# Seven quarter products for the last four MLP blocks of an attention and MLP kernel

## The chip, the cores and the metric

The kernel runs on one core of one Trainium2 chip. The metric is the time of the program on the device in microseconds (us), median over runs; lower is better. Before: 1475.31 us, median of three runs (1474.25 to 1478.08).

In the profiles PE is the matrix engine and PEld its loading of weights, DVE is the vector engine, ACT the scalar engine and POOL a fourth one; PSUM is the memory that matmuls add into, in banks. A record is one instruction of the trace; each matmul of the MLP shows as two records (2304 of hT in the page of before, for 18 blocks of 64 matmuls). Tile names: sc is the scores, xT the attention weights times V (a "weighing"), hT a piece of h, g its Gelu, o_ps the second MLP product, and bank a PSUM tile of the changed kernel.

## The reference, cut to what matters

Attention with a threshold (batch 8, 8 heads, 576 tokens, head size 64), then a two-layer MLP with exact Gelu over the 4608 tokens. All data is 32-bit floating point in the kernel; the MLP weights come in as 64-bit and are converted there.

```python
scores = scale * np.matmul(q, k.transpose(0, 1, 3, 2))
thresh = np.max(scores, axis=-1, keepdims=True) - tau
scores = np.where(scores >= thresh, scores, -1000000000.0)
attn = softmax(scores)                            # cut
x = (attn @ v).transpose(0, 2, 1, 3).reshape(4608, 512)
h = x @ w_in                                      # 512 x 2048
g = 0.5 * h * (1.0 + erf(h * inv_sqrt2))
return g @ w_out                                  # 2048 x 512
```

## The kernel before

Attention goes in 160 slots: a pair of heads, 128 rows at a time. In each slot the MLP fills the rest of PE's time: `fill` emits MLP matmuls until a "goal", a number of MLP blocks that should be done by then, is met. A block is 256 tokens; there are 18.

```python
def block_steps(n):
    g = {}
    for j in range(N_DF):                          # 16 chunks of d_ff
        if j % 2 == 0:
            hT = None
        for c in range(N_DM):                      # 4 pieces of d_model
            yield NS_IN, (j * P // PIECE + 1) * N_DM
            if hT is None:
                hT = ps.tile([P, 2, TOK], FP32, tag="mm", name="hT")
            nc.tensor.matmul(hT[:, j % 2, :], lhsT=w_in_sb[c][:, j * P:(j + 1) * P], rhs=x_blk[n][:, c, :],
                             start=(c == 0), stop=(c == N_DM - 1))
        if j % 2:
            late.append((g, j, hT))
            gelus(lag[0])                          # up to 2 Gelus stay unissued until the next slot
    for m in range(TOK // P):
        for j in range(N_DF):
            ...                                    # cut
            nc.tensor.matmul(o[:, 0:d_model], lhsT=g[j][:, m * P:(m + 1) * P], rhs=w_out_sb[j],
                             start=(j == 0), stop=(j == N_DF - 1))
        ...                                        # copy to o_sb, write out

GOAL += [(BATCH * (m + 2) + WEIGH, x) for m, x in enumerate([1.96, 3.96, 5.96, 8.06, 10.16, 12.26, 14.36])]
...
for n in range(len(slots) + WEIGH + 1):
    if p < NP:
        scores(p, i)
        softmax_head(p, i)
    gelus(0)                                       # the Gelus left over from the slot before
    table()
    if p > EARLY and i == WEIGH:                   # attention weights times V for the pair before:
        for h in range(2):                         # each half takes one of the four "mm" buffers of PSUM
            weigh_v(p - 1, h * HALF, (h + 1) * HALF)
    ...                                            # softmax_tail, transposes
    fill(owed, tokens)
fill(1e12, B * S)                                  # what is left of the MLP: the tail
```

## Time and profile before

| | before |
|---|---|
| timed runs | 1475.31 us (1474.25 to 1478.08) |
| span of the profile | 1472.4 us |
| PE, DVE, ACT busy | 97%, 63%, 44% |
| last attention matmul ends | 1264.8 us |
| plain MLP after it | 203.8 us |

The prediction below shows the busy shares, the slices and the chain. Two lines of the groups and one of the groups by form complete them. The columns are line, engine, operation, output and inputs, shapes and count, then busy us and the mean ns of one, then the idle time before them.

```profile
L468 PE MATMUL hT<-x,w_in 128*128 128x256 f32 x2304 | 518.7, 382 | 0.0
L480 PE MATMUL o_ps<-w_out,g 128*128 128x512 f32 x1152 | 517.8, 600 | 0.0
...
L428 ACT COPY x<-xT 128x256 f32<-128x256 f32 x20 | 7.4, 371 | 0.8 <-PE xT L419 0.8
```

Both MLP products have no idle time before them, and they overlap: the 382 and 600 ns of one are longer than the distances at which they start (215.9 and 429.2 ns, from the chain). A matmul's price is therefore read from the chain or from a long window, not from the mean of one.

### The profile page before, as it was taken

Reading aid. Unit: us, or ns where it says so; the run is one execution under the profiler, and the core shown is the slowest. Engines: PE = TensorE matmul, PEld = TensorE weight load, DVE = VectorE, ACT = ScalarE, POOL = GpSimd, SP = SyncE. Lnnn points to the kernel's source line nnn. Section 1 sums busy time; section 2 is a strip of 40 time slices with the busy share of each in tenths; the row PEclk is TensorE's granted clock in tenths of the full one; section 3 lists DMA queues with packets and bytes.
Section 4 is the critical chain, followed back from the end, with each engine's and each line's share of the span. In section 5 each row is a group of like instructions: output and inputs, shape, how many; then the busy total and the mean of one; then the engine's idle time right before and its main releaser. Section 6 shows DMA issues by size and latency. Waiting matters only on the chain.

```text
span 1472.4 us, 18592 instructions
## 1 busy us (share of the span) xinstructions
PE 1429.3 (97%) x6288; PEld 904.8 (61%) x6288; DVE 931.8 (63%) x2098; ACT 642.6 (44%) x1014; POOL 294.3 (20%) x502
## 2 busy tenths in 40 slices
PE   6899899999999999999999999999999999999998
PEld 5576447465665657474747575656656665675774
DVE  5988889987777777766676767776766765000000
ACT  5768536546263626352434444354535263210110
POOL 3221324322222222112222222212122000000000
PEclk9999999999999999999999999999999999999999
DMA  9876468886565556556666655545566444000000
GB/s 286 258 262 170 122 118 134 140 143 103 102 107 98 100 100 104 101 89 110 112 112 113 112 103 82 106 86 105 86 112 105 95 81 86 10 15 15 0 15 14
DMA packets 421292, 155.11 MB, mean 105 GB/s; under 512 B 399952, under 2 KB 404624, under 8 KB 421200
## 3 DMA queue, kind: packets, MB, share of 16 engines
q1 hardware_dynamic: 394992, 96.77, 38.8%
q0 software_dynamic: 23808, 56.57, 14.8%
q8 instruction: 51, 0.84, 0.2%
q10 hardware_dynamic: 2400, 0.59, 0.2%
q14 instruction: 41, 0.34, 0.1%
HBM read 61.85 MB, written 9.44 MB: 48 GB/s over the span
## 4 chain that ended last, share of the span: by engine, by line
PE 85%; DVE 7%; ACT 4%; DMA 2%; SPq 2%; issue 1%; DVEq 0%; ACTq 0%
PE o_ps L480 33%; PE hT L468 31%; PE sc L340 11%; PE xT L419 9%; DVE nmx L351 2%; DVE p L365 1%; DMA q<-in_q_dram 1%; ACT p L352 1%; ACT L448 1%; SPq L228 1%; DVE power L176 1%; PE tr L286 1%; DVE pd L393 1%; ACT L455 1%; DMA pT<-pd 0%
## 5 line engine op out<-in xcount | busy, mean ns | idle before, releaser
L468 PE MATMUL hT<-x,w_in 128*128 128x256 f32 x2304 | 518.7, 382 | 0.0
L480 PE MATMUL o_ps<-w_out,g 128*128 128x512 f32 x1152 | 517.8, 600 | 0.0
L468 PEld LDWEIGHTS hT<-x,w_in 128*128 128x128 f32 x2304 | 432.9, 190 | 88.4 <-issue 31.0
L352 ACT ACTIVATE p<-sc,nmx 128x576 f32<-128x576 f32 x288 | 203.2, 741 | 515.9 <-DVE nmx L351 515.8
L480 PEld LDWEIGHTS o_ps<-w_out,g 128*128 128x128 f32 x1152 | 215.2, 191 | 260.9 <-issue 257.7
L351 DVE TENSOR_REDUCE nmx<-sc 128x1 f32<-128x576 f32 x288 | 205.7, 751 | 234.3 <-PE sc L340 234.1
L365 DVE SCALAR_TENSOR_TENSOR p<-sc,thr,p 128x576 f32<-128x576 f32 x288 | 225.4, 816 | 33.1 <-ACT p L352 19.9
L210 POOL DMA_DIRECT2D q<-in_q_dram x104 | 70.0, 679 | 647.5 <-DVE q_tail L328 401.9
L340 PE MATMUL sc<-kT,qT 64*128 64x288 f32 x960 | 158.0, 435 | 14.6 <-DVE p L365 14.3
L419 PE MATMUL xT<-pT,v 128*64 128x288 f32 (+2 forms) x1280 | 165.2, 411 | 4.8 <-ACT g L448 4.8
L393 DVE STREAM_TRANSPOSE pd<-p 128x576 f32<-128x576 f32 x224 | 160.4, 754 | 1.7 <-ACT p L379 1.3
L340 PEld LDWEIGHTS sc<-kT,qT 64*128 64x128 f32 x960 | 87.7, 188 | 91.5 <-issue 76.1
L419 PEld LDWEIGHTS xT<-pT,v 128*64 128x64 f32 x1280 | 90.7, 137 | 75.4 <-issue 14.7
L381 DVE TENSOR_SCALAR p<-p,rden 128x576 f32<-128x576 f32 x240 | 120.2, 536 | 4.9
L218 POOL DMA_DIRECT2D v<-in_v_dram x208 | 111.1, 536 | 60.4 <-DMA k<-in_k_dram 35.4
L448 ACT ACTIVATE g<-hT 128x512 f32<-128x512 f32 x144 | 82.2, 596 | 80.9 <-PE hT L468 79.9
L448 ACT ACT_TABLE_LOAD x81 | 103.9, 1283 | 1.4
L455 ACT ACT_TABLE_LOAD x80 | 102.6, 1283 | 1.4
L483 ACT COPY o_sb<-o_ps 128x512 f32<-128x512 f32 x36 | 20.9, 582 | 138.1 <-PE o_ps L480 134.1
L210 POOL DMA_DIRECT2D k<-in_k_dram x104 | 72.7, 705 | 0.0
L286 PE MATMUL tr<-diag,p 128*128 128x128 f32 (+1 forms) x360 | 47.9, 296 | 8.5 <-ACT g L448 4.6
L286 PEld LDWEIGHTS tr<-diag,p 128*128 128x128 f32 (+1 forms) x360 | 40.7, 190 | 17.7 <-ACT g L448 6.0
(74 smaller groups left out, 551.8 us busy)
## 6 DMA issues: line engine op xcount, KB each, us to landing
pT<-pd SPq DMA_DIRECT2D x448, 160.0 KB, 4.8
out_dram<-o_sb SPq DMA_DIRECT2D x36, 256.0 KB, 2.5
pT<-pd_tail SPq DMA_DIRECT2D x112, 80.0 KB, 2.9
q<-in_q_dram POOLq DMA_DIRECT2D x104, 72.0 KB, 4.6
k<-in_k_dram POOLq DMA_DIRECT2D x104, 72.0 KB, 6.2
v<-in_v_dram POOLq DMA_DIRECT2D x156, 40.0 KB, 5.0
raw<-in_moe_w_out_dram POOLq DMA_DIRECT2D x10, 512.0 KB, 5.5
shifted<-in_moe_w_out_dram POOLq DMA_DIRECT2D x10, 511.5 KB, 5.5
```

The costliest lines, as they stand in the source:

```text
L210: eng.dma_start(t[e * D + f:e * D + f + Q], rows[:, :, f:f + Q])
L340: nc.tensor.matmul(sc[e][:, h, 0:HALF], lhsT=lhsT, rhs=s["kT"][rows, at:at + HALF], start=True, stop=True)
L351: nc.vector.tensor_reduce(nmx[:, e:e + 1], sc, axis=AXIS.XY, op=ALU.max, negate=True)
L352: nc.scalar.activation(w[:, e * S:(e + 1) * S].rearrange("p (h s) -> p h s", h=2), sc, AF.Exp, bias=nmx[:, e:e + 1], scale=1.0)
L365: nc.vector.scalar_tensor_tensor(row, sc[e][:, :, 0:HALF], thr[:, e:e + 1], row, op0=ALU.is_ge, op1=ALU.mult, accum_out=den[:, e:e + 1])
L381: nc.vector.tensor_scalar(row, row, rden[:, e:e + 1], None, op0=ALU.mult)
L393: nc.vector.transpose(to[:, 0:NB, :], w[:, e * S:(e + 1) * S].rearrange("p (b i) -> p b i", i=Q))
L419: nc.tensor.matmul(xT[f, 0:hi - lo], lhsT=s["v"][:, e, c, :], rhs=pT[:, c, lo:hi], start=(c == 0), stop=(c == KR - 1))
L448: nc.scalar.activation(t, hT, AF.Gelu)
L455: nc.scalar.activation(warm[:, 1:2], warm[:, 0:1], AF.Exp)
L468: nc.tensor.matmul(hT[:, j % 2, :], lhsT=w_in_sb[c][:, j * P:(j + 1) * P], rhs=x_blk[n][:, c, :], start=(c == 0), stop=(c == N_DM - 1))
L480: nc.tensor.matmul(o[:, 0:d_model], lhsT=g[j][:, m * P:(m + 1) * P], rhs=w_out_sb[j], start=(j == 0), stop=(j == N_DF - 1))
```

## The change

The last four blocks go two at a time (512 tokens) through Strassen's algorithm in Winograd's form: each of the two matrix products is cut into quarters, and seven quarter products replace eight, at the price of additions on DVE and copies on ACT. Several quarter results share a partial sum, so a PSUM bank is read half-way and then added to again. The sums of w_in, the quarters of g and the rest get no memory of their own: they live in tiles that attention no longer needs. The goals of the fill are lowered, as only 14 blocks are plain.

```diff
+    PLAIN = N_BLK - 4
...
-                if n == N_BLK or (n + 1) * TOK > tokens:
+                if n == PLAIN or (n + 1) * TOK > tokens:
...
+    def product(to, pairs, start=False):
+        for k, (l, r) in enumerate(pairs):
+            nc.tensor.matmul(to, lhsT=l, rhs=r, start=start and k == 0, stop=k == len(pairs) - 1,
+                             skip_group_check=not start)
...
+        def finish_chunk(j, x, p3):
+            product(x, p3)
+            nc.scalar.activation(g21(j), x, AF.Gelu)
+            vec.tensor_tensor(gs1(j), g21(j), g22(j), op=ALU.add)
+            vec.tensor_tensor(gs2(j), gs1(j), g11(j), op=ALU.subtract)
+            vec.tensor_tensor(g21(j), g11(j), g21(j), op=ALU.subtract)
...
+            for j in range(NJ):
+                x, y = bank("sc")[:, 0:TOK], bank("mm")[:, 0:TOK]
+                product(x, [(lhs_in(c, j, 0), a[:, c, :]) for c in ks], True)
+                nc.scalar.copy(g11(j), x)
+                product(y, [(lhs_in(c, j, 1), b[:, c, :]) for c in ks], True)
+                nc.scalar.copy(g22(j), y)
+                if prev:
+                    finish_chunk(*prev)
+                product(x, [(lhs_ext(s2, c, j), t2[:, c, :]) for c in ks])
+                nc.scalar.copy(g12(j), x)
...                                     # second product into y, v_ of its own
+                product(x, [(lhs_ext(s1, c, j), t1[:, c, :]) for c in ks])
+                vec.tensor_tensor(g22(j), g22(j), x, op=ALU.add)
+                nc.scalar.activation(g22(j), g22(j), AF.Gelu)
+                if sb == 0:
+                    w_out_sums(j)
+                prev = j, x, [(lhs_ext(s4, c, j), b[:, NK + c, :]) for c in ks]
+            finish_chunk(*prev)
...
+            for m in ms:
+                vs[m] = bank("mm")[:, 0:HD]
+                product(vs[m], rows(g12, m, w_out_part(1, 0)), True)
...                                     # six more products of the second stage, outputs
-    GOAL += [... enumerate([1.96, 3.96, 5.96, 8.06, 10.16, 12.26, 14.36])]
+    GOAL += [... enumerate([1.96, 3.96, 5.96, 7.97, 9.98, 11.99, PLAIN])]
...
+        elif n == len(slots):
+            ext = weights_in()          # 12 sums of w_in on DVE
...
     fill(1e12, B * S)
+    strassen(PLAIN, *ext)
```

More of the change, by code (lines that the diff above doesn't have):

```diff
@@ L504, in fill, with units, unit @@
             mlp["next"] = next(mlp["steps"], None)
+    HF = d_ff // 2
+    NJ = HF // P
+    HD = d_model // 2
+    NK = HD // P
+    U = 512
+    vec = nc.vector
+    def units(t):
+        flat = t.rearrange("p a b -> p (a b)") if len(t.shape) == 3 else t.rearrange("p a b c -> p (a b c)")
+        return [flat[:, k * U:(k + 1) * U] for k in range(flat.shape[1] // U)]
+    def unit(pool, tag, n=1):
+        t = pool.tile([P, n, U], FP32, tag=tag, name="unit")
+        return [t[:, k, :] for k in range(n)]
@@ new lines, in weights_in @@
+    def weights_in():
+        room = [x for tag in ("q", "k", "qT", "kT") for _ in range(2) for x in unit(ld, tag)]
+        room += unit(work, "p", 2) + unit(work, "p", 2)
+        rest = [units(v_sb[i % 4])[0] for i in range(NP - 4, NP - 1)]
+        s1, s2, s4 = ({} for _ in range(3))
+        for h in range(HF // U):
+            lo, hi = slice(h * U, (h + 1) * U), slice(HF + h * U, HF + (h + 1) * U)
+            for c in range(NK):
+                for to in (s1, s2, s4):
+                    to[c, h] = room.pop(0)
+                vec.tensor_tensor(s1[c, h], w_in_sb[c][:, hi], w_in_sb[NK + c][:, hi], op=ALU.add)
+                vec.tensor_tensor(s2[c, h], s1[c, h], w_in_sb[c][:, lo], op=ALU.subtract)
+                vec.tensor_tensor(s4[c, h], w_in_sb[NK + c][:, lo], s2[c, h], op=ALU.subtract)
+        return (s1, s2, s4), room + rest
@@ new lines, in strassen, with quarter, lhs_in, lhs_ext @@
+    def strassen(first, ext, room):
+        s1, s2, s4 = ext
+        n_sb = (N_BLK - first) // 2
+        for h in range(HF // U):
+            for c in range(NK):
+                a = w_in_sb[c][:, HF + h * U:HF + (h + 1) * U]
+                vec.tensor_tensor(a, w_in_sb[c][:, h * U:(h + 1) * U], a, op=ALU.subtract)
+        room = room + units(v_sb[(NP - 1) % 4]) + [u for t in pd_tail for u in units(t)]
+        room += [x for _ in range(2) for x in unit(xg, "x", 2)]
+        x_ext = [room.pop().rearrange("p (c t) -> p c t", c=NK) for _ in range(3)]
+        o_ext = [room.pop() for _ in range(2)]
+        room += [x for _ in range(N_DF // 2 + 3) for x in unit(gp, "g")]
+        room += [u for t in pd for u in units(t)]
+        room += [x for e in range(2) for x in unit(one, f"pT{e}", 5)]
+        def quarter():
+            got = [room.pop(0).rearrange("p (j t) -> p j t", t=TOK) for _ in range(NJ // 2)]
+            return lambda j: got[j // 2][:, j % 2, :]
+        g11, g12, g21, g22, gs1, gs2 = (quarter() for _ in range(6))
+        wt1, wt2, wt4 = (quarter() for _ in range(3))
+        def lhs_in(c, j, hi):
+            at = (HF if hi else 0) + j * P
+            return w_in_sb[c][:, at:at + P]
+        def lhs_ext(t, c, j):
+            return t[c, j * P // U][:, j * P % U:j * P % U + P]
+        def product(to, pairs, start=False):
+            for k, (l, r) in enumerate(pairs):
+                nc.tensor.matmul(to, lhsT=l, rhs=r, start=start and k == 0, stop=k == len(pairs) - 1,
+                                 skip_group_check=not start)
+        def bank(tag):
+            if tag == "sc":
+                return ps.tile([P, 2, 512], FP32, tag="sc", name="bank", bufs=2)[:, 0, :]
+            return ps.tile([P, 512], FP32, tag="mm", name="bank")
+        def x_sums(n):
+            t1, t2, t4 = x_ext
+            a, b = x_blk[n], x_blk[n + 1]
+            b11, b21, b12, b22 = a[:, 0:NK, :], a[:, NK:2 * NK, :], b[:, 0:NK, :], b[:, NK:2 * NK, :]
+            vec.tensor_tensor(t1, b12, b11, op=ALU.subtract)
+            vec.tensor_tensor(t2, b22, t1, op=ALU.subtract)
+            vec.tensor_tensor(b12, b22, b12, op=ALU.subtract)
+            vec.tensor_tensor(t4, b21, t2, op=ALU.subtract)
+        def w_out_sums(j):
+            b11, b12 = w_out_sb[j][:, 0:HD], w_out_sb[j][:, HD:2 * HD]
+            b21, b22 = w_out_sb[NJ + j][:, 0:HD], w_out_sb[NJ + j][:, HD:2 * HD]
+            vec.tensor_tensor(wt1(j), b12, b11, op=ALU.subtract)
+            vec.tensor_tensor(wt2(j), b22, wt1(j), op=ALU.subtract)
+            vec.tensor_tensor(b12, b22, b12, op=ALU.subtract)
+            vec.tensor_tensor(wt4(j), b21, wt2(j), op=ALU.subtract)
+        def finish_chunk(j, x, p3):
[4 more added lines that the diff above has]
+            vec.tensor_tensor(g21(j), g11(j), g21(j), op=ALU.subtract)
+        x_sums(first)
+        for sb in range(n_sb):
+            n = first + 2 * sb
+            t1, t2, t4 = x_ext
+            a, b = x_blk[n], x_blk[n + 1]
+            ks = range(NK)
+            prev = None
+            for j in range(NJ):
[8 more added lines that the diff above has]
+                nc.scalar.copy(g12(j), x)
+                product(y, [(lhs_in(NK + c, j, 1), t4[:, c, :]) for c in ks])
+                vec.tensor_tensor(g12(j), g12(j), y, op=ALU.add)
+                nc.scalar.activation(g12(j), g12(j), AF.Gelu)
+                v_ = bank("mm")[:, 0:TOK]
+                product(v_, [(lhs_in(NK + c, j, 0), a[:, NK + c, :]) for c in ks], True)
+                vec.tensor_tensor(g11(j), g11(j), v_, op=ALU.add)
+                nc.scalar.activation(g11(j), g11(j), AF.Gelu)
+                product(x, [(lhs_ext(s1, c, j), t1[:, c, :]) for c in ks])
[5 more added lines that the diff above has]
+            finish_chunk(*prev)
+            ms = range(TOK // P)
+            def rows(g, m, w):
+                return [(g(j)[:, m * P:(m + 1) * P], w(j)) for j in range(NJ)]
+            def w_out_part(k, d):
+                return lambda j: w_out_sb[k * NJ + j][:, d * HD:(d + 1) * HD]
+            vs, xs, ys = ([None] * len(ms) for _ in range(3))
+            lo = [op.tile([P, d_model], FP32, tag="o_sb", name="o_sb") for _ in ms]
+            hi = o_ext
+            for m in ms:
+                vs[m] = bank("mm")[:, 0:HD]
+                product(vs[m], rows(g12, m, w_out_part(1, 0)), True)
+            for j in range(NJ):
+                vec.tensor_tensor(g12(j), g12(j), gs2(j), op=ALU.subtract)
+            for m in ms:
+                xs[m] = bank("sc")[:, 0:HD]
+                product(xs[m], rows(g11, m, w_out_part(0, 0)), True)
+                nc.scalar.copy(lo[m][:, 0:HD], xs[m])
+                vec.tensor_tensor(lo[m][:, 0:HD], lo[m][:, 0:HD], vs[m], op=ALU.add)
+            if sb + 1 < n_sb:
+                x_sums(n + 2)
+            for m in ms:
+                ys[m] = bank("mm")[:, 0:HD]
+                product(ys[m], rows(g21, m, w_out_part(0, 1)), True)
+                nc.scalar.copy(hi[m][:, HD:2 * HD], ys[m])
+            for m in ms:
+                product(xs[m], rows(gs2, m, wt2))
+                nc.scalar.copy(hi[m][:, 0:HD], xs[m])
+            for m in ms:
+                product(ys[m], rows(g22, m, wt4))
+                vec.tensor_tensor(hi[m][:, 0:HD], hi[m][:, 0:HD], ys[m], op=ALU.add)
+            for m in ms:
+                product(xs[m], rows(gs1, m, wt1))
+                vec.tensor_tensor(hi[m][:, HD:2 * HD], hi[m][:, HD:2 * HD], xs[m], op=ALU.add)
+                row = (n + 1) * TOK + m * P
+                nc.sync.dma_start(out[row:row + P, :], hi[m])
+            for m in ms:
+                product(xs[m], rows(g12, m, w_out_part(1, 1)))
+                nc.scalar.copy(lo[m][:, HD:2 * HD], xs[m])
+                row = n * TOK + m * P
+                nc.sync.dma_start(out[row:row + P, :], lo[m])
@@ L524 @@
     GOAL = [(-1, 0.0), (START - 1, 0.0), (BATCH - 1, 0.55)]
-    GOAL += [(BATCH * (m + 2) + WEIGH, x) for m, x in enumerate([1.96, 3.96, 5.96, 8.06, 10.16, 12.26, 14.36])]
+    GOAL += [(BATCH * (m + 2) + WEIGH, x) for m, x in enumerate([1.96, 3.96, 5.96, 7.97, 9.98, 11.99, PLAIN])]
     def goal(n):
```

## The prediction

An addition of 128x256 on DVE: the trace of after shows 0.42 us for one (L635), so 2.5 us for the six of a chunk and 4.2 us for the ten of a chunk in the first half, beside 6.04 us of PE. The forecast's sum came to -27.0 - 0.2 + 4.0 = -23.2 us, 1452.1 us.

> **What bounds the kernel now.** I read the page's busy shares and slices first, then the chain of waits, the waits of PE, and the windows and the timeline of the last 230 us. From the page:
>
> ```profile
> PE 1429.3 (97%) x6288; PEld 904.8 (61%) x6288; DVE 931.8 (63%) x2098; ACT 642.6 (44%) x1014; POOL 294.3 (20%) x502
> ...
> PE   6899899999999999999999999999999999999998
> PEld 5576447465665657474747575656656665675774
> DVE  5988889987777777766676767776766765000000
> ```
>
> PE is full from the fourth slice (some 110 us) on; DVE runs at seven tenths beside it and has nothing to do in the last six slices. Busy PE need not be PE at its peak, so I looked for real waits. The waits of PE between 640 and 1270 us are one line:
>
> ```profile
> PE xT L419 <- ACT g L448: 4.8, 3, 1.6
> ```
>
> So in 630 us PE waits three times, 1.6 us each; otherwise attention and MLP matmuls follow each other without a hole. PE's stream is the bound, both in the attention loop and in the tail; work taken off PE comes off the time. The chain of waits, in order of time over the last 270 us, gives the price of the MLP:
>
> ```profile
> 1243.00 16.84 PE hT L468 x78
> 1259.84 5.00 PE xT L419 x40
> 1264.84 10.99 PE hT L468 x50
> 1275.83 27.47 PE o_ps L480 x64
> 1303.30 27.63 PE hT L468 x128
> 1330.92 27.47 PE o_ps L480 x64
> ```
>
> The last attention work is the xT group that ends at 1264.84. One plain block of 256 tokens is 27.63 + 27.47 = 55.10 us: 128 records of hT (two for each of the 64 matmuls of the program) at 215.9 ns, and 64 records of o_ps (32 matmuls) at 429.2 ns. The window of one whole block says how much room stands beside it:
>
> ```profile
> 1358.39:1413.48 55.09, 55.09 (x193) 36.48 (x193) 0.00 (x0) 5.95 (x10) 0.00 (x0) 1.00 0.03 10
> ```
>
> (Columns: stretch, length, busy PE, PEld, DVE, ACT, POOL, granted clock, DMA share, GB/s.) The clock is full, DVE idle, ACT busy 6 us of 55. Strassen's additions have free engines to go to.
>
> [...]halving the columns of the second product from 512 to 256 costs almost nothing (2 x 215.9 = 431.8 against 429.2), provided that the weight load (190 ns in the page's PEld groups) still hides behind 215.9, as it does in hT. [...]The kernel before has no tensor_tensor, but its two-input operations on 128x512 (L176, L178) take 685 to 688 ns[...]. [...]The change needs that: it reads a bank half-way and goes on adding to it. No run yet shows it.
>
> **The change part by part.**
>
> *Removed.* Blocks 14 to 17 in plain form: 4 x 55.10 = 220.4 us of PE. In the kernel before, 0.36 of block 14 stands inside the attention loop (its goal ends at 14.36) and the rest in the tail. The new goal ends at 14, so the loop loses 0.36 x 55.1 = 20 us of fill. Because PE is the bound there too, I count the loop as that much shorter and charge all four blocks at one price.
>
> *Added on PE.* For 512 tokens the first product has 7 quarter products x 8 chunks x 2 matmuls = 112, the second 7 x 2 x 8 = 112, all 128x256. 224 x 2 records x 215.9 ns = 96.7 us for two blocks instead of 110.2; for four blocks 193.4 us. **Net on PE: 220.4 - 193.4 = 27.0 us less.**
>
> *Added on DVE and ACT in the tail.* Per chunk, 7 products take 7 x 2 x 0.4318 = 6.0 us on PE. ACT has three copies and four Gelus of 128x256; the copy L428 of that shape takes 371 ns, so 7 x 0.37 = 2.6 us. [...]They also fit in order: a bank that was read and is continued is reached one or two products (0.86 us each) after the product that filled it, and a read needs about 0.1 us to start and 0.37 to run. The tightest is the first chunk, where x is continued straight after y: the copy has 0.86 us for about 0.5. One Gelu table load (1283 ns in the ACT groups) falls into the same chunk, on ACT, ahead of a Gelu that PE needs only in the second product. I count no stall. In the second product each bank is continued at least 3.45 us after it was read.
>
> *Added at the seam.* The 12 sums of w_in (12 x 0.69 = 8.3 us) come on DVE after the last transposes; the trace of before has DVE idle there from 1246.3 us and the last xT starts at 1259.8, so they and the four in-place differences (2.8 us) end before it. The sums of x need the last copies of xT (some 0.55 us after xT ends); the third of them, which the second product (y) waits for, ends at about 0.55 + 3 x 0.72 = 2.7 us. In PE's order of the changed kernel three o_ps matmuls (3 x 0.858 = 2.6 us) and the product x1 (0.86 us) stand between, 3.4 us. Hidden, with 0.7 us to spare.
>
> *End.* The last copy before the last output is 128x256 instead of 128x512: 0.37 against 0.58 us, so 0.2 us less.
>
> *Moved.* This is what the diff does not show. A weighing of V (xT) takes two PSUM buffers of the four of "mm". If it falls into an hT stage with one hT half filled and two whose Gelu is issued only in the same slot, its second half waits for that Gelu. In the order of instructions of the kernel before I find this pattern in exactly three slots, 87, 142 and 152, and the trace has exactly three such waits. The lower goals make almost exactly two blocks per batch of 20 slots, so the phase between blocks and weighings no longer drifts, and in the order of the changed kernel the pattern stands in five slots: 117, 127, 137, 147, 157. What one costs:
>
> ```profile
> 1099.38 2.65 PE L419 MATMUL xT<-pT,v 128*64 128x288 f32 x20
> 1103.64 2.82 PE L419 MATMUL xT<-pT,v 128*64 128x288 f32 x20 [1.61 <-ACT g L448]
> 1106.39 3.29 PE L468 MATMUL hT<-x,w_in 128*128 128x256 f32 x14
> ```
>
> From start to the next group 1106.39 - 1099.38 = 7.0 us, against 5.0 for an undisturbed weighing (the 5.00 in the chain above): 2.0 us each. Two more: **+4.0 us.**
>
> *Sum.* -27.0 - 0.2 + 4.0 = -23.2; 1475.3 - 23.2 = 1452.1 us, a gain of 1.6%.
>
> **The rivals.**
> 1. *The seven products are dense, and the two extra waits don't come or are made up.* Speaks for it: the pattern was counted, not timed, and waits shift with the phase. It gives 1475.3 - 27.2 = 1448.1 us. Even the whole arithmetic gain is 1.85%, short of 2%.
> 2. *PE starts to wait for the vector engines inside Strassen.* Banks are read and continued, every product waits for an ACT or DVE result, and only two "sc" banks serve x. Against it: the margins above[...]. If each of the 16 chunks lost 0.5 us, it would be 8 us: 1460 us.
> 3. *The attention loop doesn't get shorter with less fill,* because its own chain (scores, maximum, exp, comparison) takes over. In an early slot of before the next sc waits for the comparison L365 (nine such waits, all before 290 us). Against it: in the late loop sc starts at 1208.31 and the last comparison of that slot ends at 1212.9, while the next sc comes at 1215.69, 2.8 us later; the change takes 0.25 us off a mean slot, and the batches between goals 1.96 and 5.96 already run at two blocks a batch without a wait. If it were so, 20 us less would come back: some 1470 us.
> 4. *256-column second products expose weight loads.* 190 against 215.9 ns and hT's dense 215.9 speak against it; with 190 ns exposed now and then it would be a few us.
>
> **Range and chances.** The middle is 1452 us: the fixed arithmetic and two more Gelu waits. Below, rival 1 ends at 1448, and I allow 0.5 us of noise. Above, I allow 5.5 us for small stalls in the first chunk, at the seam and between the products. So 1447.5 to 1457.5. Faster by over 2% would need less than about 1446 us, more than the arithmetic has: 4%. Slower by over 2% would need more stalls than the whole gain twice over: 1%.
>
> **What would show each step.** The page's groups should have 896 records of the new product line, at starts 215.9 ns apart, and 1792 of hT and 896 of o_ps. Strassen, from its first to its last matmul, should take 193 to 194 us with PE full and the clock at 1.00; 200 or more, with waits of PE for ACT or DVE in it, is rival 2. The waits of PE for Gelu in xT should be five of 1.6 us. The last xT should end some 15 us earlier than 1264.84 (16.84 of hT and three o_ps of 0.86 less ahead of it, 4 more of waits); if it ends where it did, rival 3. DVE should be about 8 us busy between the last transposes and xT, and PE without a hole at the seam. The prediction is wrong if a wait that I didn't count, such as a release of memory that attention leaves (pd, pT, v), stands at the start of Strassen.

## The result, and the profile after

| | before | after |
|---|---|---|
| median, runs of the first comparison | 1475.84 us (4 runs) | 1457.0 us (1455.29 to 1458.31, 4 runs) |
| ratio, 95% interval | | 0.9871, 0.9853 to 0.9888 |
| ratio in the repetition below, 5 runs | | 0.9849, 0.9836 to 0.9863 |
| span of the profile | 1472.4 us | 1453.5 us |
| DVE, ACT busy | 931.8, 642.6 us | 1009.5, 663.1 us |

A ratio is the mean time of one kernel's runs over that of the other's of the same rounds, so it is not quite the ratio of the medians. Every run whose record names a check was correct (after_again is the changed kernel). The gain is clear of noise, but below 2%.

The busy shares and slices of the page after:

```profile
PE 1405.4 (97%) x6416; PEld 930.5 (64%) x6416; DVE 1009.5 (69%) x2278; ACT 663.1 (46%) x1096; POOL 291.8 (20%) x502
...
PE   6899989999999999999999999999999999999999
PEld 5576546556574747575656656574747565688887
DVE  5988888987777777777777776767767676562230
```

PE stays full to the end; DVE now has work in the last slices: six tenths in the slice that holds most of the first stage of Strassen's first half (1271.8 to 1308.2 us), two to three tenths in the three after it. The waits of PE between 640 and 1460 us (total, times, longest):

```profile
PE xT L420 <- ACT g L449: 8.1, 5, 1.6
PE bank L578 <- DVE unit L635: 1.0, 2, 0.5
```

The first line is the five weighings of the prediction (three before). The second is new: PE waits twice for a DVE addition in Strassen. The chain of waits from the last weighing to the end shows where (start, us, what):

```profile
1247.21 5.00 PE xT L420 x40
1252.21 2.77 PE o_ps L481 x6
1254.98 47.50 PE bank L578 x220
1302.48 0.02 issue
1302.50 0.43 DVE unit L635
1302.93 0.04 issue
1302.98 96.97 PE bank L578 x448
...
1400.45 49.49 PE bank L578 x228
1449.94 0.02 issue
1449.97 0.37 ACT o_sb L682
```

Strassen runs from 1254.98 to 1449.94, 195.0 us, where 896 records at 215.9 ns would be 193.4. The first piece is dense (47.50 us for 220 records is 215.9 ns each); the second, in which all products of the second stage of the first half stand, has 216.5 ns each, so 256-column second products are nearly as dense as hT (without any wait they are as dense: see strassen_both). The 1.5 us that remain are two places, 96.97 + 0.5 us apart: the end of the first stage in each half. Each is 0.5 us of wait and some 0.27 us in the piece after it (448 records at 215.85 ns would be 96.70 us). The timeline tells why. First an inner chunk, then the last one (start, us, engine, line; the bracket is the idle time before and what ended it):

```profile
1290.21 1.89 PE L578 MATMUL bank<-x,w_in 128*128 128x256 f32 x8
1290.42 0.42 DVE L635 TENSOR_TENSOR unit<-unit,bank 128x256 f32<-128x256 f32 x1 [0.44 <-PE bank L578]
...
1291.94 1.03 PE L578 MATMUL bank<-x,unit 128*128 128x256 f32 x4
```

```profile
1301.44 1.03 PE L578 MATMUL bank<-unit 128*128 128x256 f32 x4
...
1302.50 0.42 DVE L635 TENSOR_TENSOR unit<-unit,bank 128x256 f32<-128x256 f32 x1 [0.44 <-PE bank L578]
...
1302.98 1.13 PE L578 MATMUL bank<-x,unit 128*128 128x256 f32 x4 [0.51 <-DVE unit L635]
```

In an inner chunk eight records of the next chunk (its x and y) stand between the product that L635 reads and the one that goes on adding to the same bank, and L635's 0.42 us hide behind them. In the last chunk there is no next one: the code calls `finish_chunk` at once, and PE has to wait until DVE has read the bank. The weight load waits with it and starts only with the matmul, at 1302.98; in the inner chunk it is ahead (1291.73 and 1291.94 us). That fits the 0.27 us; no run isolates it.

The first look (1457.0) lies 4.9 us above the prediction (1452.1). The two waits are 1.5 us of that, and 0.5 us is the kernel before, whose median was 1475.84 in this comparison and not 1475.31; some 3 us remain. Before the experiments I compared the two traces scores group by scores group. Goals and tail differ only later, yet at one group the profile of before is at 409.7 us and that of after at 412.4 us. I call this group slot 60, here and in the expectations below; that is a miscount, as by the program's own count it is the 57th of the 160 slots (index 56). The slots of the prediction (87, 142, 117 and so on) are by the program's count. Every run is measured at the same group, so no difference suffers from the name. In the windows from 200 us on, granted clock is the third column from the end: here the first profile of before,

```profile
200.00:220.00 20.00, 20.00 (x98) 10.99 (x97) 16.49 (x38) 7.38 (x14) 0.66 (x2) 0.98 0.47 93
220.00:240.00 20.00, 18.52 (x88) 14.68 (x87) 18.12 (x42) 11.77 (x16) 9.51 (x16) 1.00 1.07 176
```

and here the changed kernel:

```profile
200.00:220.00 20.00, 20.00 (x94) 10.79 (x93) 14.94 (x35) 6.99 (x13) 0.00 (x0) 0.93 0.36 74
220.00:240.00 20.00, 18.53 (x80) 13.92 (x77) 16.89 (x37) 9.23 (x13) 9.47 (x16) 0.91 1.11 179
```

The clock was lower here in one than in the other (0.93 against 0.98, then 0.91 against 1.00), at the same work. PE is busy for the whole first window in both, with 98 records in before and 94 in after: busy was not the same as full speed here. Whether that was chance or the change's doing was left to the experiments.

### The profile page after: what moved, and what is told of

The parts are those of the page before. It is cut to its first block, busy times and chain, and to the rows that moved or that the text cites. A ratio compares the mean times of both kernels' runs of the same rounds, so it can differ in the third digit from the quotient of the medians.

```text
span 1453.5 us, 19183 instructions
## 1 busy us (share of the span) xinstructions
PE 1405.4 (97%) x6416; PEld 930.5 (64%) x6416; DVE 1009.5 (69%) x2278; ACT 663.1 (46%) x1096; POOL 291.8 (20%) x502
## 4 chain that ended last, share of the span: by engine, by line
PE 86%; DVE 7%; ACT 5%; issue 1%; DMA 1%; SPq 0%; DVEq 0%; ACTq 0%
PE o_ps L481 26%; PE hT L469 25%; PE bank L578 13%; PE sc L341 11%; PE xT L420 9%; DVE nmx L352 2%; DVE p L366 2%; ACT p L353 1%; ACT L449 1%; PE tr L287 1%; DVE power L177 1%; ACT L456 1%; DVE pd L394 0%; ACT g L449 0%; DVE w_in L179 0%
## 5 line engine op out<-in xcount | busy, mean ns | idle before, releaser
L469 PE MATMUL hT<-x,w_in 128*128 128x256 f32 x1792 | 408.7, 383 | 0.0
L481 PE MATMUL o_ps<-w_out,g 128*128 128x512 f32 x896 | 407.5, 603 | 0.0
L469 PEld LDWEIGHTS hT<-x,w_in 128*128 128x128 f32 x1792 | 336.1, 190 | 73.8 <-issue 28.3
L481 PEld LDWEIGHTS o_ps<-w_out,g 128*128 128x128 f32 x896 | 167.1, 191 | 201.4 <-issue 198.5
L341 PE MATMUL sc<-kT,qT 64*128 64x288 f32 x960 | 159.5, 439 | 12.6 <-DVE p L366 12.3
L449 ACT ACTIVATE g<-hT 128x512 f32<-128x512 f32 x112 | 63.2, 596 | 0.9
L429 ACT COPY x<-xT 128x256 f32<-128x256 f32 (+7 forms) x124 | 28.1, 285 | 51.0 <-PE xT L420 50.9
```

What stands on the lines that cost most here:

```text
L341: nc.tensor.matmul(sc[e][:, h, 0:HALF], lhsT=lhsT, rhs=s["kT"][rows, at:at + HALF], start=True, stop=True)
L449: nc.scalar.activation(t, hT, AF.Gelu)
```

## The experiments

My theory: PE is the bound from start to end, so each part of the change counts for what it does to PE's stream: -27.2 us for the seven products and the shorter last copy, +1.5 for two waits on DVE, +4.0 for two more weighings that wait for a Gelu; the rest of the miss is the early clock, which is chance. Rivals: the loop doesn't get shorter with less fill, as its own chain takes over; the vector work is on the path; the changed kernel is slower early for a cause of its own.

As the first 400 us wander, I quote for each run, beside the ratio, the time from slot 60 to the end in its profile. Differences in the text are taken before rounding.

| run | median us | ratio to before, 95% interval | slot 60 at | slot 60 to end |
|---|---|---|---|---|
| before, first profile | | | 409.7 | 1062.7 |
| after, first profile | 1457.0 | 0.9871 (0.9853 to 0.9888) | 412.4 | 1041.1 |
| goals_only | 1481.36 | 1.0026 (1.0013 to 1.0038) | 414.9 | 1066.8 |
| plain_no_gelu_wait | 1469.75 | 0.9952 (0.9940 to 0.9965) | 410.3 | 1056.7 |
| strassen_no_gelu_wait | 1445.2 | 0.9784 (0.9771 to 0.9797) | 411.8 | 1031.1 |
| strassen_both | 1443.9 | 0.9776 (0.9762 to 0.9789) | 414.1 | 1029.5 |
| before_again | 1477.8 | 1.0001 (0.9989 to 1.0014) | 413.9 | 1062.6 |
| after_again | 1455.87 | 0.9849 (0.9836 to 0.9863) | 412.6 | 1041.2 |
| last_chunk | 1456.17 | 0.9848 (0.9832 to 0.9865) | 413.9 | 1039.6 |
| extra_adds | 1449.06 | 0.9799 (0.9781 to 0.9818) | 411.9 | 1035.2 |

The kernel before had a median of 1477.57 us beside the four runs from goals_only to strassen_both and 1477.23 us beside the last four.

### goals_only: the new goals alone, tail plain

```diff
-    ... enumerate([1.96, 3.96, 5.96, 8.06, 10.16, 12.26, 14.36])]
+    ... enumerate([1.96, 3.96, 5.96, 7.97, 9.98, 11.99, 14])]
```

> The kernel before with only the new goals of the fill (7.97, 9.98, 11.99, 14 in place of 8.06, 10.16, 12.26, 14.36), tail plain. My theory: all of the loop's share of the change is two more weighings that wait for a Gelu (five instead of three), 2.0 us each: 4.0 us slower than the kernel before, some 1480 us, with five waits of 1.6 us in the waits of PE and the last xT at 20 us less fill plus 4. Rival (the loop does not get shorter with less fill, or the early part is slower for a reason of its own in the changed kernel): clearly more than 4 us slower, 7 us or more.

Measured: 3.8 us slower than before by the medians, 4.1 us from slot 60 to the end. The waits of PE:

```profile
PE xT L419 <- ACT g L448: 8.1, 5, 1.6
```

Five waits, as counted from the order of instructions beforehand. Against this kernel, which has the changed kernel's loop and a plain tail, the changed one is 1066.8 - 1041.1 = 25.7 us shorter from slot 60 on: -27.2 of arithmetic and +1.5 of waits, to a tenth of a microsecond. The loop did get shorter by what was taken out of it.

### plain_no_gelu_wait: the kernel before with goals that avoid the waits

```diff
-    ... enumerate([1.96, 3.96, 5.96, 8.06, 10.16, 12.26, 14.36])]
+    ... enumerate([1.96, 3.96, 5.96, 7.96, 9.96, 11.96, 13.96])]
```

These goals were found by building several variants and counting in their order of instructions the weighings that meet a half filled hT and two unissued Gelus; with these there are none.

> The kernel before, plain tail, with goals (7.96, 9.96, 11.96, 13.96) for which the order of instructions has no weighing that meets a half filled hT and two unissued Gelus. My theory: the three waits of before go, 3 x 2.0 = 6 us faster than the kernel before, 1470 us, no wait of PE after 300 us. Rival (the waits are made up elsewhere, by sc waiting for the comparison or by hT waiting for its buffers): within 2 us of the kernel before.

Measured: 5.9 us less from slot 60 to the end, 7.8 us by the medians (the interval of the ratio is 5 to 9 us). PE waits for nothing after 640 us. Three waits were worth 2.0 us each: 1.6 us idle, and some 0.4 us more. In the trace of before the weight load of the second half starts only with its matmul after the wait (1103.63 and 1103.64 us), which fits those 0.4; no run isolates them.

### strassen_no_gelu_wait: the changed kernel with those goals

> The changed kernel with the same goals (7.96, 9.96, 11.96, 13.96). My theory: five waits of 2.0 us go, 10 us faster than the changed kernel: 1447 us; and against the plain kernel with the same goals it is faster by the pure difference of the tails, 27.0 + 0.2 - 1.5 = 25.7 us. Rival: the loop's chain takes back most of it, 1453 us or more.

Measured: 10.1 us less than the changed kernel from slot 60 on, five waits of 2.0 us; and 25.7 us less than the plain kernel with the same goals. The median was 1445.2 us, faster than the 1447 expected, the ratio 0.9784.

### strassen_both: and the last chunk's third product moved

```diff
-            finish_chunk(*prev)
             ms = range(TOK // P)
...
             for m in ms:
                 vs[m] = bank("mm")[:, 0:HD]
                 product(vs[m], rows(g12, m, w_out_part(1, 0)), True)
+            finish_chunk(*prev)
```

The first product of the second stage needs g12 alone, which is done by then, so it can stand between.

> The same, and the last chunk's third product (the one into x that must wait until DVE has read x) stands behind the first product of the second stage in both halves. My theory: the two waits of 0.5 us for DVE with their exposed weight loads go: 1.5 us faster than the run with the goals alone, 1445.5 us; Strassen from its first to its last matmul takes 193.4 to 193.6 us. Rival (Strassen is 1.5 us longer than counted for another cause, spread over it): 195 us remain.

Measured: 1.6 us less from slot 60 to the end. The chain of waits:

```profile
1246.64 193.40 PE bank L578 x896
1440.04 0.02 issue
1440.07 0.37 ACT o_sb L681
```

All of Strassen is one piece of 193.40 us, 896 records at 215.8 ns, with no wait for anyone. The version is the fastest: 1443.9 us, ratio to the kernel before 0.9776.

### before_again and after_again: the two kernels once more

> The kernel before unchanged, for a second profile and as the zero of the comparison. My theory: the first 400 us, which all these kernels share, wander by some us from run to run with the granted clock (0.83 to 1.00 in slices there), while from slot 60 to the end the time is fixed: 1062.7 us in the first profile, and again within 0.3 us here; ratio to its own runs 1.000 within 0.001. Rival (the fixed part wanders as well): it differs by over 1 us.

> The changed kernel unchanged. My theory: the part from slot 60 to the end is 1041.1 us again, 21.5 us less than before; so the true ratio is about 1 - 21.6 / 1476 = 0.985, and the 0.987 of the first look was low by the wandering of the first 400 us in four runs. Rival (the changed kernel is slower in the first 400 us for a cause of its own): the ratio is 0.987 again, and the time up to slot 60 is longer than that of the kernel before in every profile.

Measured: from slot 60 to the end both kernels repeat within 0.1 us of their first profiles (1062.6 and 1041.2). The time up to slot 60 does not: the kernel before took 409.7 us in one profile and 413.9 in the other, and over all ten profiles, which share the program up to there, it lies between 409.7 and 414.9. The first profile of before is the shortest of them. The second profile of before shows the lower clock too, in the same windows:

```profile
200.00:220.00 20.00, 20.00 (x86) 10.29 (x87) 14.96 (x34) 7.73 (x15) 1.57 (x4) 0.89 0.40 86
220.00:240.00 20.00, 18.53 (x82) 13.69 (x80) 17.10 (x37) 9.45 (x14) 9.46 (x16) 0.91 1.06 176
```

So the early difference was not the change's doing. The ratio of the repetition, 0.9849, agrees with what 21.5 us less on 1477 give (0.9854).

The traces say more about the early part than I used. In the first profiles of before and of after the recorded clock there is 1.00 or 0.50, and nothing between (a window that holds both shows their mean); the low stretches are 3.4 or 6.8 us long. In both, one begins within 0.7 us of the end of an idle gap of PE of 2.8 us near 195 us. Some 0.4 us after a gap of 1.5 us near 229 us another begins in after, and none in before. All ten profiles have both gaps. The six sc records that follow the second one take 1.21 us in the first profile of before and in plain_no_gelu_wait, and 1.85 to 2.05 us in the eight others. One window in the first profiles of before and of after:

```profile
230.20:233.60 3.40, 3.40 (x17) 3.01 (x16) 2.97 (x7) 2.70 (x4) 1.40 (x3) 1.00 1.27 241
```

```profile
230.20:233.60 3.40, 3.40 (x11) 2.14 (x8) 2.94 (x6) 3.37 (x6) 2.01 (x4) 0.50 1.27 205
```

From the 21st to the 57th slot the first profile of before takes 245.9 us with 3.4 us at half clock, and that of after 249.2 us with 10.2; plain_no_gelu_wait takes 247.2 us and the seven others 249.1 to 249.2 us. I estimate from the recorded 0.50 that 6.8 us more at half clock cost 3.4 us; the difference between before and after is 3.3. So the first profile of before gained 3.3 us on that of after here; at the 21st slot it had been 0.7 us behind. The rest of the wander lies before the 21st slot, which starts between 162.8 and 165.7 us.

### last_chunk: the moved product alone

> The changed kernel with only the last chunk's third product moved behind the first product of the second stage, the goals as in the change. My theory: 1.5 us faster than the changed kernel (0.5 us of wait and 0.3 us of exposed weight load, twice), five weighings still waiting 1.6 us each, no wait for DVE in Strassen. Rival: less than 0.5 us, as the wait moves to the next product.

Measured: 1.6 us less from slot 60 to the end (1039.6 against 1041.2), five weighings still waiting and no wait in Strassen. The timed medians do not show it (1456.17 and 1455.87 us): the intervals are wider than the effect, and this run's slot 60 came 1.2 us later. By the timed runs alone (1456.14 to 1456.35, and one of 1451.38) this experiment would have been inconclusive.

### extra_adds: eight more additions per chunk on DVE

```diff
                 if sb == 0:
                     w_out_sums(j)
+                for _ in range(8):
+                    vec.tensor_tensor(scratch, w_out_sb[N_DF - 1][:, 0:TOK], w_out_sb[N_DF - 1][:, TOK:2 * TOK], op=ALU.add)
```

> The version with both repairs and eight more additions of 128x256 per chunk on DVE, into dead memory, results unchanged. A chunk is 6.04 us of PE; an addition took 0.42 us in the trace. My theory (the vector work of Strassen lies wholly beside PE): in the second half 6 + 8 = 14 additions are 5.9 us and still fit, so that half does not change; in the first half 6 + 4 + 8 = 18 are 7.6 us and DVE becomes the bound, 8 chunks x 1.6 = 12 to 13 us more; in all 1456 to 1458 us. Rival (the additions are already on the path, by their order or by memory they share with PE): both halves get longer, 8 x 8 x 0.42 = 27 us or more for each half.

The additions come on top of strassen_both. Measured: 5.7 us more than strassen_both from slot 60 on, all of it in the first half; 5.2 us by the medians, though one of its four timed runs, which has no profile, took 1443.54 us and the others 1448.93 to 1449.46. The waits of PE, and the last PE piece of the chain:

```profile
PE bank L578 <- DVE unit L636: 4.2, 5, 0.8
```

```profile
1293.08 150.50 PE bank L578 x696
```

PE waits five times, all in the first half; from 1293.08 on, with 14 additions per chunk in the second half, it runs 696 records without a hole (150.50 / 696 = 216.2 ns). So 14 additions fit beside a chunk, more than twice the 6 that the second half needs, and 18 do not: the vector work is off the path, with room. My size (12 to 13 us) was more than twice too large, for two reasons that the trace shows. In the first half the chunk that DVE bounds takes 7.14 us, not the 7.6 of 18 x 0.42:

```profile
1279.80 0.42 DVE L601 TENSOR_TENSOR unit<-w_out,unit 128x256 f32<-128x256 f32 x1
1280.13 3.63 DVE L641 TENSOR_TENSOR scratch<-w_out 128x256 f32<-128x256 f32 x8
1283.68 0.42 DVE L606 TENSOR_TENSOR pd<-unit 128x256 f32<-128x256 f32 x1
1284.13 0.42 DVE L607 TENSOR_TENSOR pd<-pd,v 128x256 f32<-128x256 f32 x1
...
1287.27 3.63 DVE L641 TENSOR_TENSOR scratch<-w_out 128x256 f32<-128x256 f32 x8
```

An addition is recorded as 0.42 us, but one that does not read the result of the one before it starts 0.33 to 0.35 us after it; where it does, as L607 after L606, it is 0.45. The eight extra ones, which all write one tile, start 0.44 us apart on average (3.55 us for eight), so the time was saved by the ten others (3.59 us). And DVE could fall behind for some chunks before PE felt it: in the eight chunks PE waited five times.

## Why the prediction was right or wrong

**What bounds the kernel** was right. Every term that was taken off or put on PE's stream, in the loop or in the tail, showed in the time: +4.1, -5.9, -10.1 and -1.6 us in the runs that changed one at a time.

**The arithmetic of Strassen** was right: 27.0 us from 4 x 55.10 less 193.4, and 193.40 was measured where nothing waits. The end was 0.2 us shorter, as predicted (0.37 against 0.59 us for the last copy). Rival 4, exposed weight loads, is refuted by the same piece. It also shows what no run had shown before, matmuls that go on in banks which ACT or DVE has read in between: the results were correct, and the 896 records stay 215.8 ns apart.

**The moved part** was right, in number (three, then five) and in size: predicted 2.0 us each, measured 4.1 for two, 5.9 for three, 10.1 for five. Rival 1, two extra waits that don't come, is refuted with it: they came in the five slots that were counted.

**The step that failed** is "a bank that was read and is continued is reached one or two products (0.86 us each) after the product that filled it", and with it "I count no stall". It holds for the inner chunks, whose third product waits behind the next chunk's x and y; it does not hold for the last chunk in each half, where the loop ends and the code continues the bank at once. I had looked for the tightest place at the start (the first chunk, which didn't wait) and not at the loop's end. The price was 1.5 us in all, small beside the range. Rival 2, PE waiting for the vector engines inside Strassen, came true in these two places alone; its size, 8 us, is refuted by the dense pieces, and extra_adds shows how much room the other chunks have. A slip beside it: the 3.45 us of the second product count from the end of the product that fills the bank, not from the read; nothing waited there.

**The seam** was right in its outcome, with one wrong detail: the sums of x don't need the last copies of xT. The tokens of the first half of the last weighing suffice, and in the trace of after the sums end at 1251.97, before xT itself ends (1252.21).

**Rival 3**, a loop that doesn't get shorter, is refuted by goals_only: the same loop with the plain tail costs two waits and nothing else. The last xT ended 12.6 us earlier in the first pair of profiles and 16.4 in the second, predicted 15; counted from slot 60, it is 15.3 and 15.2.

**The time.** With the missed 1.5 us the sum is 1453.6 us on the first median; the repetition's ratio gives 0.9849 x 1475.3 = 1453.0. The 1457.0 of the first look lay at the upper edge of the range for a reason that the prediction named only as 0.5 us of noise: the first 400 us wander by 5 us. Between the first profiles of before and after, 3.3 us of that stand where after has 6.8 us more at half clock. The interval of the first ratio is 3.5 thousandths, 5 us, wide, so it says so itself. That it still lay inside the range was in part luck: the 5.5 us above the middle were meant for stalls, which took 1.5, and the wander took most of the rest. Why the same idle gap is followed by half clock in one run and not in another stays open.

## What to carry to other kernels

When PE is full everywhere, price a change from PE's stream alone, but also count in the order of instructions which waits its new schedule creates or removes: here the phase between two interleaved loops was worth 10 us, more than a third of Strassen's gain, and a goal moved by 0.01 to 0.04 blocks took it away. Where a bank is read and then added to again, check the first and the last pass of the loop, as what hides the read in the middle can be missing there; here the last pass waited and the first did not. To see an effect of a thousandth, compare a stretch of the profile that repeats (here slot 60 to the end, equal within 0.1 us) and not only the whole time, which wandered here by up to 5 us.
